# Loading the first weights from a second queue, turning the first rows by ordinary products, and an even last cut

## The chip, the cores and the metric

The kernel runs on one core of one Trainium2 chip. The time is device time of one execution, in microseconds; the kernel before was run three times (679.69, 679.70 and 680.63, median 679.7), and once more under the profiler (679.49, of which 677.7 are the profile's span).

## The reference

Two layers read the same x (2048 rows of 1024, bfloat16), and a gate mixes their results row by row.

```python
def _A_ref(x, wqkv, wo):            # attention, 32 heads of 32, window 8, step 2
    qkv = x @ wqkv
    ...
    attn = softmax(masked logits)
    return (sum over the window of attn * v) @ wo

def _B_ref(x, w_in, w_sp, b_sp, w_out):
    z = gelu(x @ w_in)              # w_in: 1024 x 3584
    z1, z2 = z[:, :1792], layernorm(z[:, 1792:])
    return (z1 * (w_sp @ z2 + b_sp)) @ w_out

g = sigmoid((x * gate_w).sum(-1))
out = g * _A_ref(x) + (1 - g) * _B_ref(x)
```

## The kernel before, in words

Everything on SBUF lives in one large tile, `arena`, in which regions are named and reused. PSUM is one pool of eight banks, tag `ps`. The kernel is written under a manual schedule: each engine runs its instructions in the order in which the program writes them, and each waits on semaphores for what it reads. TensorE goes through long runs of matrix products: x by the second half of w_in (line 300), x by wqkv (lines 621 and 644), x by the first half of w_in (line 809), w_sp by z2 (lines 836 and 910), and then the two output products, with w_out (line 1038) and with wo (lines 1117 and 1127).

The change touches the two ends.

*The front.* TensorE multiplies with the contraction on the partitions, so x is needed with its columns on the partitions: `xT`, of which each row tile of 128 rows has eight pieces of 128 columns (`kt`, eight row blocks of w_in). Row tiles 2 to 15 are turned by DMA (`dma_start_transpose`, line 523). Row tiles 0 and 1 are loaded as they lie, into `xn` (line 514), and turned by TensorE in `z2_quad` (line 316), four pieces to a PSUM bank; VectorE (line 320) and ScalarE (line 322) copy two pieces each into `xT`. While x's first tile is on its way, TensorE runs `warm_up`: seven products of constants (line 100).

`z2_quad` then makes four output banks at once: row tiles 0 and 1 (`i`) by column chunks 0 and 1 (`c`, 512 columns each) of w_in's second half. It runs over the eight row blocks `kt`, and in each over `c` and then `i`, so 32 products of 128x128 by 128x512. Block 0 comes in two transfers, one for each column chunk (line 516); blocks 1 to 7 come in one transfer each of 128 x 1024 values, 256 KB (line 518). Behind the quad, row tile 2 is taken up, then 3 and so on (`z2_tile`).

All these transfers are issued by SyncE, one after the other. A transfer tells of its landing by one of eight semaphores in turn, and each issue waits until the transfer eight places before it has landed.

*The end.* `both_pairs(7)` makes the last 256 output rows. The last product, `product4(..., a22, wo_sums[3], ...)` (lines 1190 to 1193), is done in two column parts of the last half row: 384 columns in the bank `apb`, and 128 in `apd`, into which ScalarE copied `apb`'s last 128 columns before (line 1176). VectorE's `combine` (line 1107) scales each part by the gate and adds it to `mix`, which ScalarE writes from the bank `mpb` just ahead (line 1181); SyncE stores each part by itself (line 1193).

## Time and profile before

| what | value |
|---|---|
| median of three runs | 679.7 us |
| the profiled execution | 679.49 us |
| its span | 677.7 us |
| TensorE busy | 673.0 us, 99% |
| VectorE busy | 558.4 us, 82% |
| ScalarE busy | 415.8 us, 61% |
| warm-up products | 0.78 to 3.61 us |
| x's first two tiles turned | 3.42 to 5.17 us |
| first product of line 300 | 5.69 us |
| last product of line 1127 begins to end | 673.23 to 674.27 us |

Times in the profile are counted from the start of the span. A row of the timeline shows start, length, engine, line, operation, output and input and the number of merged instructions; what stands in brackets is the idle time of the engine before it and what ended that. A row of the chain of waits shows start, length and what ran or was waited for. A row of a group shows output and input, form and count, then busy time in us, the mean of one in ns, and idle time before them. "PE" is TensorE's product, "PEld" its weight load, "SPq" and "ACTq" the issue of a transfer by SyncE and by ScalarE.

## The change

w_in's row block 0 becomes one transfer of 256 KB and is issued by ScalarE; the other seven stay with SyncE. Row tiles 0 and 1 are turned by ordinary products with the identity matrix in place of transposes, with float32 banks in place of bfloat16 ones. Row tile 0 is turned first and multiplied with block 0, then row tile 1 is turned, and the other products follow in the order tile 0 block 1, tile 1 blocks 0 and 1, and from block 2 on tile 0 and tile 1 in turn. At the end, the last product is cut into 256 and 256 columns, and ScalarE's copy ahead of it takes 256 columns.

```diff
     def z2_quad():
-        for i in range(2):
+        def turn(i):
             for h in range(2):
-                pt = psum.tile([P, 4, P], BF, name="pt", tag="ps")
+                pt = psum.tile([P, 4, P], F32, name="pt", tag="ps")
                 for k in range(4):
-                    nc.tensor.transpose(pt[:, k, :], xn[:, i, (4 * h + k) * P:(4 * h + k + 1) * P], ident[:])
+                    nc.tensor.matmul(pt[:, k, :], xn[:, i, (4 * h + k) * P:(4 * h + k + 1) * P], ident[:],
+                                     start=True, stop=True)
...
-        quad = [[psum.tile([P, 512], F32, name="ps", tag="ps") for c in range(2)] for i in range(2)]
-        for kt in range(KT):
+
+        turn(0)
+        quad = [[psum.tile([P, 512], F32, name="ps", tag="ps") for c in range(2)]]
+        order = [(0, 0), (0, 1), (1, 0), (1, 1)] + [(i, kt) for kt in range(2, KT) for i in range(2)]
+        for i, kt in order:
             for c in range(2):
-                for i in range(2):
-                    z2_mm(quad[i][c], i, c, kt, ZW[c])
+                z2_mm(quad[i][c], i, c, kt, ZW[c])
+            if (i, kt) == (0, 0):
+                turn(1)
+                quad.append([psum.tile([P, 512], F32, name="ps", tag="ps") for c in range(2)])
...
-    for c in range(2):
-        sync.dma_start(w2[c][:, 0, :], win_v[:, 0, FH + ZC * c:FH + ZC * (c + 1)])
-    for kt in range(1, KT):
-        sync.dma_start(w2_01[:, kt, :], win_v[:, kt, FH:FH + 2 * ZC])
+    for kt in range(KT):
+        queue = nc.scalar if kt == 0 else sync
+        queue.dma_start(w2_01[:, kt, :], win_v[:, kt, FH:FH + 2 * ZC])
...
         if q == 7:
             apd = bank()
-            nc.scalar.copy(apd[:, 384:512], apb[:, 384:512])
+            nc.scalar.copy(apd[:, 256:512], apb[:, 256:512])
...
-            for ps, n0, nw in ((apb, 0, 384), (apd, 384, 128)):
+            for ps, n0, nw in ((apb, 0, 256), (apd, 256, 256)):
                 product4(ps[:, n0:n0 + nw], a22, wo_sums[3][:, :, n0:n0 + nw], False)
                 combine(b, ps[:, n0:n0 + nw], n0, nw)
                 sync.dma_start(out2[b * P:(b + 1) * P, n0:n0 + nw], ob_slots[b % 4][:, n0:n0 + nw])
```

## What was predicted

> **What bounds the kernel now.** I read the page first, then the chain of waits in order of time, for its first 36 us and its last 5, then the timeline of those two stretches.

> ```profile
> span 677.7 us, 8946 instructions
> PE 673.0 (99%) x3311; PEld 355.1 (52%) x3311; DVE 558.4 (82%) x667; ACT 415.8 (61%) x765; POOL 29.4 (4%) x62
> PE 99%; DMA 1%; SPq 0%; ACT 0%; DVE 0%; issue 0%; DVEq 0%
> ```

> TensorE is busy for 673.0 of 677.7 us and makes up 99% of the chain. All that the change can win lies at the two ends, and the first is a DMA wait:

> ```profile
> 1.65 4.00 DMA arena<-in_B_w_in_dram
> 5.65 0.04 issue
> 5.69 1.02 PE ps L300 x4
> 6.71 0.02 issue
> 6.73 28.65 PE ps L300 x132
> ```

> Columns: start, length, what. The first half of w_in's row block 0 is issued at 1.65 and lands at 5.65; the first product of line 300 starts at 5.69. Four products later TensorE waits once more (the fifth starts at 6.73), then it runs without a hole at 28.65/132 = 0.217 us a product. The timeline of the same stretch:

> ```profile
> 0.73 1.28 ACT L322 ACT_TABLE_LOAD   x1 [0.73 <-PEq L1303]
> 0.74 0.87 SPq L514 DMA_DIRECT2D arena<-in_A_x_dram  x2
> 0.78 2.83 PE L100 MATMUL pw<-const-bfloat16-1.0 128*128 128x512 bf16 x7 [0.78 <-PEq L1303]
> 1.65 0.91 SPq L516 DMA_DIRECT2D arena<-in_B_w_in_dram  x2
> 2.60 3.40 SPq L518 DMA_DIRECT2D arena<-in_B_w_in_dram  x7
> 3.42 1.58 PEld L316 LDWEIGHTS <-arena 128*128 128x128 bf16 x16 [0.41 <-DMA arena<-in_A_x_dram]
> 3.42 1.75 PE L316 MATMUL pt<-ident,arena 128*128 128x128 bf16 x16
> 4.07 1.44 DVE L320 COPY arena<-pt 128x256 bf16<-128x256 bf16 x4 [4.07 <-PE pt L316]
> 4.39 1.52 ACT L322 COPY arena<-pt 128x256 bf16<-128x256 bf16 x4 [2.38 <-DVE arena L320]
> 6.06 9.22 SPq L523 DMA_TRANSPOSE arena<-in_A_x_dram  x5
> 12.50 2.57 DVE L528 TENSOR_REDUCE o_l<-arena 128x1 f32<-128x1024 bf16 x2 [4.74 <-DMA arena<-in_A_x_dram]
> ```

> x's first tile releases the turns at 3.42; the 16 turns are through at 5.17, and TensorE idles 0.52 us. The row at 12.50 is VectorE released by row tile 2, the first that a DMA turns: it has landed by 12.50. TensorE takes it up a little later:

> ```profile
> 12.34 0.81 PE L300 MATMUL ps<-arena 128*128 128x512 bf16 x3
> ```

> That is the 31st and 32nd product of the quad and then the first of tile 2, which starts at 12.34 + 2 x 0.217 = 12.77. So the front of the kernel is two races: TensorE reaches the end of its quad at 12.77, and the DMA stream delivers tile 2 at 12.50, only 0.27 us ahead. Mean DMA rates by stretch (last two columns: busy share, GB/s):

> ```profile
> 3.00:3.50 0.50, 0.50 (x4) 0.09 (x3) 0.00 (x0) 0.00 (x0) 0.02 (x1) 1.00 1.03 397
> 3.50:4.00 0.50, 0.50 (x7) 0.50 (x7) 0.00 (x0) 0.00 (x0) 0.00 (x0) 1.00 0.48 96
> 4.00:4.50 0.50, 0.50 (x8) 0.50 (x6) 0.29 (x2) 0.11 (x1) 0.00 (x0) 1.00 0.55 139
> 4.50:5.00 0.50, 0.50 (x8) 0.50 (x7) 0.37 (x2) 0.44 (x2) 0.00 (x0) 1.00 0.98 256
> 5.00:5.50 0.50, 0.18 (x3) 0.06 (x2) 0.50 (x3) 0.45 (x2) 0.00 (x0) 1.00 1.09 375
> ```

> The stream drops from 397 GB/s to 96 and 139 just where the first reads of w_in begin. Against 397 it loses (301 + 258 + 141) x 0.5 = 350 KB there, 0.88 us of its own pace.

> **The change, part by part.** *w_in's row block 0.* Two 128 KB transfers, issued third and fourth on SyncE's queue (1.65, some 0.47 apart), become one of 256 KB, issued first on ScalarE's. The instruction order puts it ahead of the table load: the load that starts at 0.73 starts some 0.4 later and ends near 2.4; the first copy that needs it starts at 4.39, so that costs nothing (0.4 us at most without that cover). On SyncE's queue the seven other blocks come two places, 0.91 us, earlier. Each issue there waits for the eighth transfer before it, so what SyncE waits for moves too: block 6 now waits for block 0, block 7 for x's first tile, and the first turning transfer of line 523 for x's second tile instead of the second half of block 0 (6.06). All three come earlier than they did, if ScalarE's transfer isn't late.

> When does block 0 land? No row shows a transfer on ScalarE's queue this early. Those of line 851 do it under load, at 512 KB each:

> ```profile
> L851 ACTq DMA_DIRECT2D arena<-in_B_w_sp_dram x4: 334/356/447, 362.6 to 369.5; - x4
> DMA to landing us min/median/max: 4.9/10.7/11.0
> ```

> Lower end: beside x's first tile, landing with it at 3.42. Upper end: 4.9 us after 0.74, at 5.64. The nearest row is the chain's 4.00 us for half of the very same rows; it includes a queue that the new place does not have, but half the bytes. I take it: 0.74 + 4.00 = 4.74.

> *x's first tile* now shares the 16 engines with block 0. Lower end: 3.42, as before. Upper end: all 256 KB pass ahead of it, 0.66 us at 397 GB/s, 4.08. Since the dip says that the first reads of w_in leave the engines half idle (0.48, 0.55), x loses less than its even share; I take 3.80.

> *The turns.* Sixteen transposes become sixteen products with the same weights and the same 128 moving columns; I price them alike, 1.75/16 = 0.11 us at the early pace. That pace is half of the later one, as the two means for one shape show:

> ```profile
> L100 PE MATMUL pw<-const-bfloat16-1.0 128*128 128x512 bf16 x6 | 2.7, 624 | 0.8 <-PEq L1303 0.8
> L300 PE MATMUL ps<-arena 128*128 128x512 bf16 x384 | 86.0, 379 | 0.5 <-DMA arena<-in_B_w_in_dram 0.5
> L320 DVE COPY arena<-pt 128x256 bf16<-128x256 bf16 x4 | 1.2, 292 | 4.3 <-PE pt L316 4.1
> L605 ACT CAST arena<-ps 128x256 bf16<-128x256 f32 x16 | 5.5, 380 | 4.6 <-PE ps L621 4.6
> ```

> (Warm-ups: 2.83 us for six and a quarter, 0.43 each, against 0.217.) The granted clock of the rows above reads 1.00 throughout and doesn't show this. PSUM now holds f32; the L605 row copies the same shape from f32 in 380 ns, against 1.52/4 = 380 for the old copies, so the copies cost the same on ScalarE. For VectorE I carry the same over (its copy: 292 ns); its dearest bound is the 384-wide pass over f32 of the last fence below, 0.62, or +0.33 on the path.

> *The order.* The first two products (tile 0, block 0) now follow the first eight turns; the second eight turns come behind them, and so does everything else on TensorE if block 0 is late. Before, the first copy ended 4.07 + 0.29 = 4.36, 0.94 after the first turn; with 0.04 for the semaphore the first product can start 0.98 after it: 3.80 + 0.98 = 4.78. Block 0 asks for 4.74 + 0.04 = 4.78 as well. From there: 2 x 0.217 + 8 turns at 0.07 (between 0.055, half the early pace, and 0.11) + 30 x 0.217 = 0.43 + 0.56 + 6.51 = 7.50. The quad ends at 12.28 instead of 12.77: 0.49 gained. With x at 3.42 and block 0 no later than 4.36 it would end at 11.90 (0.87 gained), with x at 4.08 at 12.56 (0.21). The second turns' copies have two products of block 1 and x's landing ahead of them and finish inside that work.

> This stands only if the stream keeps ahead. Block 1 is needed by 4.78 + 0.43 + 0.56 = 5.77 and lands now at about 6.7 (the wait that ends at 6.73); tile 2 is needed at 12.28 and lands at 12.50. Both must come earlier, by 0.9 and 0.2 us. For tile 2 a quarter of the 0.88 us lost in the dip does it. For block 1 it takes nearly all; what is missing there is a wait at that place, and the later blocks are then ahead of it again. I count 0.10 for it: front gain 0.39.

> [...]

> *The last product* is cut 256 + 256 instead of 384 + 128:

> ```profile
> 673.43 0.70 ACT arena L1181
> 674.15 0.62 DVE arena L1107
> 674.80 0.82 SPq L1193 DMA_DIRECT2D out_dram<-arena  x2
> L1193 SPq DMA_DIRECT2D out_dram<-arena x2: 333/362/391, 674.8 to 675.2; - x2
> L1107 DVE SCALAR_TENSOR_TENSOR arena<-ps,g_s,arena 128x384 bf16<-128x384 f32 x1 | 0.6, 617 | 1.5 <-ACT arena L1181 1.5
> L1107 DVE SCALAR_TENSOR_TENSOR arena<-ps,g_s,arena 128x128 bf16<-128x128 f32 x1 | 0.3, 341 | 0.0
> L1176 ACT COPY ps<-ps 128x128 f32<-128x128 f32 x1 | 0.2, 250 | 3.4 <-DVE arena L1107 3.4
> ```

> The first combine shrinks from 617 to (617 + 341)/2 = 479 ns, so the first store is issued 0.14 earlier; the second follows 0.82 - 0.39 = 0.43 behind it, as before, and its combine (0.48) is just done by then. The last store doubles to 64 KB: 0 to 32 KB/397 GB/s = 0.08 more. Gain 0.06 to 0.14, taken as 0.10. The copy of L1176 doubles its columns, about +0.13 us; ScalarE is idle until 673.43, which hides it (uncovered it would be 0.13).

> **Sum.** 0.39 + 0.10 = 0.49. The profiled execution took 679.49 us (677.7 of span, 1.8 around it) and becomes 679.0; the median shown, 679.7, lies 0.21 above it, so the forecast is 679.2.

> **The rivals.** *One: the stream is no faster.* The bytes up to tile 2 are the same, so it still lands at 12.50, and TensorE gains at most 0.27 in front however early it starts; with the end 0.37, less what x's delay costs: 679.4. For it: the rate between 5.00 and 5.50 is already 375 GB/s. Against it: the dip is latency, not bytes (engines half idle). Chance 0.20.

> *Two: block 0 lands late on the idle queue.* In the new order TensorE can't use the wait for the second turns. The quad ends at landing + 0.04 + 7.50, so it is a loss from a landing after 5.23. At 5.64 (the least of L851): 13.18, 0.41 lost, 0.10 won at the end: 680.0. Against it: L851's transfers are twice as big and run among others. Chance 0.10.

> *Three: slower, since TensorE's full pace comes later.* The pace doubled after 4.1 us of work without a gap (from 0.78; the turns still took 0.11 in the mean, the products at 5.69 came at 0.217). The change opens a hole between the last warm-up (ends 3.61) and the first turn at 3.80 to 4.08. If a hole restarts the count, full pace comes 4.1 us after 3.80, at 7.9: from 4.78 on 3.1 us run at half pace, 1.55 us lost, less 0.49: +1.1, 680.8; it decides from a doubling after 5.8, where the loss passes the gain. At x = 4.08 it is 1.55 - 0.21 - 0.10 = +1.2, 680.9. Against it: a hole of 0.2 to 0.47 us is small, and before had one of 0.52 at 5.17 without harm, though past the doubling. [...] Chance 0.14.

> **How the numbers follow.** Forecast (gain 0.2 to 0.9) 0.51, rivals 0.20, 0.10, 0.14, and 0.05 for a spread like that of the runs shown (680.63 beside 679.69). The likeliest is 679.2, its own range 678.8 to 679.5. The range 678.5 to 680.8 takes in the best front (0.87 + 0.14 against the median: 678.7) and rival three's nearer half; about 0.12 lies outside. A difference below 0.2% (1.36 us) can't be told from none here. The whole front can't win that, so faster is 0.03, from spread alone; slower is 0.10: the half of rival three that the spread of the runs lifts over the bound (0.07), a very late block 0 (0.02), spread (0.01). Within: 0.87.

> **What would show it.** Right: the first product of line 300 near 4.8 instead of 5.69, the turns in two groups of eight about it, rates above 200 GB/s in every half microsecond from 3.0, tile 2 taken up near 12.3, the last store issued near its old time less 0.6. Wrong: a PE wait on a DMA after the quad (rival one), a first product after 5.2 (two), products 0.43 apart after 5.5 (three). A VectorE copy of clearly over 0.3 us would upset the price of the turns.

## The result, and the profile after

The kernel after takes 680.94 us (median of 22 runs, 679.80 to 681.98), the kernel before beside it 679.75 us (22 runs, 679.40 to 680.63): a ratio of 1.0016, interval 1.0009 to 1.0022. That is slower by some 1.2 us, within the 0.2% that the prediction called no change, but 0.14 us above the top of its range. The times after lie in two heaps: 6 of 22 at 679.80 to 680.03, like before, and 16 from 680.83 up. The profiled execution (681.76 us) is one of the 16; it is 2.3 us longer than that of before.

The page of the kernel after, span and busy time:

```profile
span 680.0 us, 8945 instructions
PE 674.7 (99%) x3311; PEld 355.6 (52%) x3311; DVE 559.1 (82%) x667; ACT 415.9 (61%) x765; POOL 29.4 (4%) x62
```

TensorE's busy time grew by 1.7 us for the same 3311 instructions: most of the loss isn't idle time but slower work. The chain of waits after, in order of time (start, length, what), its first 37 us:

```profile
0.74 3.79 DMA arena<-in_A_x_dram
4.53 0.05 issue
4.58 0.62 PE pt L316 x4
5.20 0.02 issue
5.22 0.43 DVE arena L321
5.66 0.05 issue
5.70 1.03 PE ps L300 x2
6.74 0.85 PE pt L316 x8
7.59 29.61 PE ps L300 x132
```

The wait that ends last in front is no longer w_in's block 0 but x's first tile, which lands at 4.53. The timeline after, the same stretch:

```profile
0.74 0.88 SPq L520 DMA_DIRECT2D arena<-in_A_x_dram  x2
0.74 0.41 ACTq L523 DMA_DIRECT2D arena<-in_B_w_in_dram  x1
0.78 2.83 PE L100 MATMUL pw<-const-bfloat16-1.0 128*128 128x512 bf16 x7 [0.78 <-PEq L1308]
4.58 1.03 PE L316 MATMUL pt<-ident,arena 128*128 128x128 bf16 x8 [0.98 <-DMA arena<-in_A_x_dram]
9.10 0.15 PEld L300 LDWEIGHTS <-arena 128*128 128x128 bf16 x1 [0.28 <-issue]
9.52 0.15 PEld L300 LDWEIGHTS <-arena 128*128 128x128 bf16 x1 [0.28 <-issue]
9.84 4.42 PEld L300 LDWEIGHTS <-arena 128*128 128x128 bf16 x21 [0.17 <-issue]
11.59 3.52 DVE L533 TENSOR_REDUCE o_l<-arena 128x1 f32<-128x1024 bf16 x3 [1.28 <-DMA arena<-in_A_x_dram]
14.59 0.81 PE L300 MATMUL ps<-arena 128*128 128x512 bf16 x3
```

Two things are to be seen. TensorE is idle for 0.98 us between its warm-up and the first turn. And its weight loads for line 300 still come 0.43 us apart at 9.10 and 9.52; only then do 21 of them fit into 4.42 us, 0.21 each. Before, products ran at that pace from 5.69 on. Tile 2 has landed by 11.59, 0.9 earlier than before, but TensorE takes it up at 14.59 + 2 x 0.217 = 15.02 instead of 12.77. This 2.25 is all of the longer span: from there to the end both kernels take 665.0 us (680.0 - 15.02 and 677.7 - 12.77 = 664.9).

## The hole and the clock

The windows give the granted clock as 1.00 throughout, but the trace also holds a record of when TensorE's clock goes from half to full, and back near the end (in before a share of 1.0 from 4.91 on and of 0.5 from 677.33, 3.06 after the last product's end; ahead of 4.91 it has no entry, and the warm-up's weight loads come 0.43 us apart). For all the profiles of this case (the experiments are told below), in us from the start of the span, with TensorE's idle time in the last window that failed to open the clock and in the one that did (time in which no product or turn ran; what lies before the span's start counts as idle):

```
kernel               full at  half at  apart    idle, window before   idle, window that opened
after                  9.73   678.74   669.01   1.07                  0.00
before                 4.91   677.33   672.42   2.70                  0.00
e1_long_warm_up        4.20   676.62   672.42   3.41                  0.00
e2_products_only       5.48   677.91   672.43   2.12                  0.06
e3_queue_only          9.67   678.68   669.01   0.84                  0.00
e4_block0_on_sync      9.54   678.55   669.01   0.90                  0.00
e5_end_only            6.14   678.56   672.42   1.46                  0.00
e6_short_warm_up       6.82   679.24   672.42   1.44                  0.34
e7_after_transposes    8.08   680.50   672.42   1.05                  0.00
e8_x0_w0_x1_fill       3.56   679.40   675.84   -                     0.62
e9_first_touch         4.19   680.02   675.83   3.41                  0.00
e10_before_filled      4.32   676.75   672.43   3.28                  0.00
e11_half_hole          3.91   679.75   675.84   -                     0.28
e12_touch_all          5.96   678.38   672.42   1.64                  0.17
```

The time between the two changes takes only three values, 669.01, 672.42 and 675.84, which lie 3.41 apart and are 196, 197 and 198 times 3.4133. So I read the openings, by estimate from these 14 profiles, as falling on a grid of 3.41 us whose phase differs from run to run: where no hole comes between, they lie anywhere from 3.56 to 6.14, though the warm-up begins at 0.77 or 0.78 (seen in 13 of the 14). The paces bear the records out: after's weight loads are 0.43 us apart up to 9.52 and 0.21 from 9.84 on, about its record at 9.73. Counting windows of 3.41 us back from each opening, the clock opened in each profile at the end of the first window in which TensorE was idle for at most 0.62 us (the most is e8's), and never at the end of one with 0.84 (e3's) or more. In after, e3, e4 and e7 the window that failed holds a hole (0.84 to 1.07 idle), in e6 a hole and the start; the others failed for the idle time ahead of the first warm-up product alone. After's windows were 2.90 to 6.31, which holds the whole hole (3.61 to 4.58), and 6.31 to 9.73, which opened it.

This also accounts for the two heaps, by estimate from these numbers: the hole does no harm only where a boundary of the grid lies between 3.57 (0.78 - 0.62 + 3.41, little enough idle before the warm-up) and 4.23 (3.61 + 0.62, little enough of the hole). That is 0.66 of 3.41, a fifth of all phases; 6 of 22 runs took no longer than before. Elsewhere the opening is put off to 7.6 to 10.4 (4.23 + 3.41, and 3.57 + 2 x 3.41). At half pace from the first product at 5.70 on, that costs half of the time up to the opening, 1.0 to 2.3 us; the upper heap, 680.83 to 681.98, lies 1.0 to 2.1 above the middle of the lower one (679.88).

## The experiments

Each was timed in five rounds (11 runs) beside the kernel before; its runs in the four groups had medians 679.84, 679.79, 679.84 and 679.77. "Above 680.3" counts the runs of the upper heap; of the 22 runs of before above, 4 lie there.

**The hole closed, x still late.** Of the kernel after, only the warm-up is longer:

```diff
-    warm_up((512,) * 6 + (128,))
+    warm_up((512,) * 8 + (256,))
```

> The changed kernel with eight and a half warm-up products of 512 in place of six and a quarter, so that TensorE works until about 4.4 us and the hole before x's first tile (lands at 4.53) is closed. Theory one (the hole of 0.98 us put off the doubling of TensorE's pace from 4.9 to 9.7): the pace doubles near 5 us again, and the time falls from 680.9 to 679.7 to 680.2; what is left over the kernel before is x's delay. Theory two (x's delay alone is the price, and the late doubling is chance): the time stays within 0.3 of 680.9 and the doubling moves at random. Theory three (products with the identity don't count as work for the clock, whatever the warm-up): the doubling stays after 8 us, the time at 680.9.

Measured: 679.77 us (679.66 to 680.15), ratio 0.9999 [0.9990, 1.0008], 0 of 11 above 680.3. Its timeline:

```profile
0.78 3.67 PE L100 MATMUL pw<-const-bfloat16-1.0 128*128 128x512 bf16 x9 [0.78 <-PEq L1308]
4.61 0.62 PE L316 MATMUL pt<-ident,arena 128*128 128x128 bf16 x8 [0.16 <-DMA arena<-in_A_x_dram]
5.97 0.61 PE L316 MATMUL pt<-ident,arena 128*128 128x128 bf16 x8
```

x comes as late as in the kernel after (4.61), but eight turns take 0.62 us instead of 1.03: the pace has doubled already. The loss is the hole's, not x's delay.

**The products alone, and the queue alone.** Both are edits of the kernel before: products into float32 banks for the transposes in their old order, or only the new transfer of block 0.

```diff
-                pt = psum.tile([P, 4, P], BF, name="pt", tag="ps")
+                pt = psum.tile([P, 4, P], F32, name="pt", tag="ps")
...
-                    nc.tensor.transpose(pt[:, k, :], xn[:, i, (4 * h + k) * P:(4 * h + k + 1) * P], ident[:])
+                    nc.tensor.matmul(pt[:, k, :], xn[:, i, (4 * h + k) * P:(4 * h + k + 1) * P], ident[:],
+                                     start=True, stop=True)
```

> The kernel before, with nothing changed but the sixteen transposes turned into products with f32 banks. Theory one: no hole, so the pace doubles near 4.9 as before; VectorE's copies take 0.42 instead of 0.29 us, hidden behind the wait for w_in: 679.6 to 679.9. Theory two: the same. Theory three: the doubling comes after 8 us and the time rises by 1 us or more, to 680.7 to 681.5.

Measured: 679.84 us (679.62 to 680.68), 1.0000 [0.9991, 1.0008], 3 of 11 above 680.3. Products or transposes: no difference.

```diff
-    for c in range(2):
-        sync.dma_start(w2[c][:, 0, :], win_v[:, 0, FH + ZC * c:FH + ZC * (c + 1)])
-    for kt in range(1, KT):
-        sync.dma_start(w2_01[:, kt, :], win_v[:, kt, FH:FH + 2 * ZC])
+    for kt in range(KT):
+        queue = nc.scalar if kt == 0 else sync
+        queue.dma_start(w2_01[:, kt, :], win_v[:, kt, FH:FH + 2 * ZC])
```

> The kernel before, with nothing changed but w_in's row block 0 as one transfer on ScalarE's queue. Theory one: x's first tile lands near 4.5, the hole opens, the pace doubles late in most runs, 680.4 to 681.4. Theory two: x lands near 4.5, sixteen turns at 0.11 end near 6.3, the quad near 13.3: +0.5, 680.2, with the doubling near 5 in the profile. Theory three: as theory two, the products are not there.

Measured: 680.82 us (679.51 to 681.54), 1.0010 [1.0001, 1.0019], 7 of 11 above 680.3. Its timeline:

```profile
0.78 2.83 PE L100 MATMUL pw<-const-bfloat16-1.0 128*128 128x512 bf16 x7 [0.78 <-PEq L1302]
4.45 1.89 PE L316 MATMUL pt<-ident,arena 128*128 128x128 bf16 x16 [0.84 <-DMA arena<-in_A_x_dram]
9.12 0.15 PEld L300 LDWEIGHTS <-arena 128*128 128x128 bf16 x1 [0.28 <-issue]
9.54 4.70 PEld L300 LDWEIGHTS <-arena 128*128 128x128 bf16 x22 [0.28 <-issue]
```

The queue by itself makes the hole (0.84) and the late doubling (9.67): this one transfer is enough for the loss, without the new order and without the products.

**Block 0 back on SyncE.** The kernel after, with `queue = sync` for all blocks, so that x comes early again.

```diff
-        queue = nc.scalar if kt == 0 else sync
+        queue = sync
```

> The changed kernel with w_in's row block 0 as one transfer, but third on SyncE's queue. x's first tile lands at 3.4, so there is no hole before the first turn; block 0 lands near 5.7 to 6.0 and the second turns stand behind it: the quad ends at 5.9 + 7.5 = 13.4, 0.6 later than before. Theory one: the pace doubles near 5 (at the latest one step later in some runs, since TensorE idles from 4.3 to 5.9), 680.2 to 680.9, with spread. Theory two: 680.3. Theory three: the doubling after 8 us, 681.5 or more.

Measured: 679.95 us, 1.0011 [1.0001, 1.0020]; six runs at 679.70 to 679.95, five at 681.28 to 682.27. Its timeline:

```profile
3.45 1.04 PE L316 MATMUL pt<-ident,arena 128*128 128x128 bf16 x8
5.38 1.01 PE L300 MATMUL ps<-arena 128*128 128x512 bf16 x2 [0.90 <-DMA arena<-in_B_w_in_dram]
9.58 4.63 PEld L300 LDWEIGHTS <-arena 128*128 128x128 bf16 x22 [0.25 <-issue]
```

x is in time (3.45), but in the new order the second eight turns can't fill the wait for block 0: the hole is only moved, to 4.48 to 5.38, and spoils the window there (0.90 idle). So a hole of that size does it in this place too, and x needn't be late. By the reckoning above, this hole does no harm for a boundary between 3.57 and 5.10 (4.48 + 0.62), 0.45 of all phases by estimate; 6 of 11 runs show no loss.

**The end alone.** The kernel before with the last product cut 256 + 256.

```diff
-            nc.scalar.copy(apd[:, 384:512], apb[:, 384:512])
+            nc.scalar.copy(apd[:, 256:512], apb[:, 256:512])
...
-            for ps, n0, nw in ((apb, 0, 384), (apd, 384, 128)):
+            for ps, n0, nw in ((apb, 0, 256), (apd, 256, 256)):
```

> The kernel before with only the last product cut 256 + 256. From the changed kernel's trace, the first combine is 0.14 shorter, but from its start to the end of the span it takes 3.6 us there and took 3.6 before: 679.6 to 679.9, no difference. By the prediction's term: 0.10 less, 679.7. A rival that puts part of the loss at the end: 680.0 or more.

Measured: 679.69 us, 0.9996 [0.9987, 1.0005]: nothing that can be told from zero, nor from the 0.10 of the prediction. The chain of waits of the kernel after shows how little is to be had:

```profile
675.68 0.70 ACT arena L1186
676.38 0.03 issue
676.40 0.48 DVE arena L1112
676.88 0.39 DVEq L1319
```

The first combine takes 0.48 instead of 0.617 us, as reckoned, but from its start to the end of the span it is 680.0 - 676.40 = 3.6 us, and before 677.7 - 674.15 = 3.55. The 0.14 is mostly given back by the second, larger store: by the trace's semaphores and counted from the first combine's start, its issue begins 0.94 later instead of 1.07, but it lands 1.61 after its issue instead of 1.52, so that the landing comes 0.04 sooner (2.55 instead of 2.59; the same 2.55 in the run of the end alone).

**A hole without touching a transfer.** The kernel before, with two warm-up products less.

```diff
-    warm_up((512,) * 6 + (128,))
+    warm_up((512,) * 4 + (128,))
```

> The kernel before with two warm-up products of 512 less: TensorE stops near 2.7 and x's first tile lands at 3.4 as before, so there is a hole of 0.7 to 0.9 us and nothing else is changed. Theory one (a hole ahead of the first turn puts the doubling of the pace off by one step): runs in two or three groups, the median 680.3 to 681.0, late doubling in the profile in half of the cases or more. Rival (only x's delay costs; chance decides the doubling): 679.8, the same spread as before.

Measured: 680.44 us (679.62 to 681.15), 1.0005 [0.9996, 1.0014], 7 of 11 above 680.3, where before beside it had 4 of 33. The interval holds 1, so the ratio alone doesn't settle it; the counts speak for a cost of the hole. Its timeline, of a run of 679.81 us:

```profile
0.77 1.97 PE L100 MATMUL pw<-const-bfloat16-1.0 128*128 128x512 bf16 x5 [0.77 <-PEq L1303]
3.50 1.89 PE L316 MATMUL pt<-ident,arena 128*128 128x128 bf16 x16 [0.75 <-DMA arena<-in_A_x_dram]
6.43 0.15 PEld L300 LDWEIGHTS <-arena 128*128 128x128 bf16 x1 [0.28 <-issue]
```

A hole of 0.75 and, with the 0.77 before the first warm-up, a window from 0.0 to 3.4 that is idle for 1.44; the products are still slow at 6.43. This profile doesn't single out the hole: 0.77 alone lies between the 0.62 and the 0.84 of above, and the opening at 6.82 costs the run little.

**After with transposes.** The kernel after, turned by transposes into bfloat16 banks again (the reverse of the first diff under "the products alone").

> The changed kernel with transposes in place of the products with the identity. Theory one: the hole is there still, 680.6 to 681.3, runs in groups as in the changed kernel. Rival (transposes don't count as work for the clock, so the products saved something): more late runs, 681.3 to 682.0. Rival (the products are what puts it off): 679.8 to 680.2.

Measured: 680.92 us (679.37 to 681.75), 1.0012 [1.0003, 1.0021], 7 of 11 above 680.3: the loss of the kernel after. By these profiles the transposes count as work for the clock: in the kernel before the window that opened it (1.49 to 4.91) holds nothing but transposes from 3.61 on, where the warm-up ends (1.30 us, which would be idle time if they didn't count, more than the 0.84 that kept a window shut), and here that of 4.66 to 8.08 holds all sixteen.

**The other order of loads.** The kernel after, everything on SyncE in the order x's first tile, block 0, x's second tile, the rest, and one warm-up product behind the first turns.

```diff
+        warm_up((512,))
...
-    for i in range(2):
-        sync.dma_start(xn[:, i, :], x_v[:, i, :])
-    for kt in range(KT):
-        queue = nc.scalar if kt == 0 else sync
-        queue.dma_start(w2_01[:, kt, :], win_v[:, kt, FH:FH + 2 * ZC])
+    sync.dma_start(xn[:, 0, :], x_v[:, 0, :])
+    sync.dma_start(w2_01[:, 0, :], win_v[:, 0, FH:FH + 2 * ZC])
+    sync.dma_start(xn[:, 1, :], x_v[:, 1, :])
+    for kt in range(1, KT):
+        sync.dma_start(w2_01[:, kt, :], win_v[:, kt, FH:FH + 2 * ZC])
```

> The changed kernel with all transfers on SyncE's queue in the order x's first tile, w_in's block 0 in one transfer, x's second tile, the other blocks; and one more warm-up product of 512 between the first eight turns and the first product of line 300. x's first tile lands at 3.4, no hole before the turns and a short one after them, so by theory one the pace doubles near 5 in nearly all runs; block 0 lands at 4.6 to 5.1, the quad ends at 5.0 + 7.5 = 12.5 against 12.77: 679.3 to 679.7. By the rival that only the stream counts (same bytes, tile 2 at 12.5): 679.5 to 679.8. Worse than 679.9: block 0 is later than 5.3 or a hole is left.

Measured: 679.76 us (679.09 to 680.42), 0.9997 [0.9988, 1.0006]. That is no faster than before, above the 679.3 to 679.7 expected and inside the range of the rival (only the stream counts): in its timeline the second turns now wait 1.41 us, for x's second tile.

```profile
6.56 0.62 PE L316 MATMUL pt<-ident,arena 128*128 128x128 bf16 x8 [1.41 <-DMA arena<-in_A_x_dram]
```

**The slow first reads of w_in.** The kernel before, with a transfer of 4 bytes of each row of block 0 first on ScalarE's queue (into a tile that nothing reads); and the same with 4 bytes of each row of all eight blocks.

```diff
+    touch = sm.tile([P, 2], BF, name="touch")
...
+    nc.scalar.dma_start(touch[:], win_v[:, 0, FH:FH + 2])
```

> The kernel before, with one more transfer ahead of everything on ScalarE's queue: four bytes of each row of w_in's block 0, into a small tile that nothing reads. It tests why the stream drops between 3.5 and 4.5. If the drop is the delay of the first reads of these rows (the theory behind w_in's share of x's delay), it is gone or halved, block 0's first half lands before 5.2, the first product of line 300 comes near 5.2 with no hole after the turns, and the time is 679.2 to 679.6. If the first reads take as long but are paid by x instead, x lands 0.3 to 1 us later and the time is 679.8 to 680.8. If the drop has nothing to do with first reads: block 0 lands at 5.3 to 5.7 as before, 679.7 to 679.9.

Measured: 679.58 us (679.17 to 680.13), 0.9993 [0.9984, 1.0002]: as expected, though the time alone can't be told from before's. The windows of this run (last two columns: DMA busy share, GB/s):

```profile
3.50:4.00 0.50, 0.50 (x6) 0.49 (x6) 0.00 (x0) 0.00 (x0) 0.00 (x0) 1.00 1.00 354
4.00:4.50 0.50, 0.44 (x6) 0.26 (x3) 0.32 (x2) 0.01 (x1) 0.00 (x0) 1.00 0.94 240
```

Where before moved 96 and 139 GB/s, it moves 354 and 240. So the dip goes with the first reads of these rows, not with the bytes; why a first read is slow, no run shows. By the trace's semaphores the first half of block 0 lands at 4.80 instead of 5.65, while x's second tile pays a part (4.51 instead of 4.00). Block 1, untouched, is then the one that is late (7.38 instead of 6.69); the timeline of the same run:

```profile
5.01 1.22 PE L300 MATMUL ps<-arena 128*128 128x512 bf16 x4
7.42 7.07 PE L300 MATMUL ps<-arena 128*128 128x512 bf16 x32 [1.19 <-DMA arena<-in_B_w_in_dram]
```

```diff
+    touch = sm.tile([P, KT, 2], BF, name="touch")
...
+    nc.scalar.dma_start(touch[:], win_v[:, :, FH:FH + 2])
```

> The kernel before with the small transfer of the last experiment taking four bytes of every row of all eight blocks of w_in. There, block 0 came 0.85 earlier, but block 1 landed at 7.4 and TensorE waited 1.2 us for it. If each block's first reads are slow once, the wait for block 1 goes too: quad 0.3 to 0.6 earlier than before, 679.1 to 679.5. If 1024 small reads hold up x instead: x's first tile lands after 4, a hole opens, 680 or more.

Measured: 679.08 us (678.87 to 679.73), 0.9991 [0.9982, 1.0000], the best median of the study, 0.7 us under before beside it; its interval ends at 1.0000, so the gain is likely rather than sure. Block 1 lands at 6.10, and in its timeline no DMA wait is left from the first product on:

```profile
5.54 9.01 PE L300 MATMUL ps<-arena 128*128 128x512 bf16 x40
```

**Before, its own hole filled.** The kernel before with two warm-up products between the turns and the first product, where it idles 0.52 us.

```diff
+        warm_up((512, 256))
```

> The kernel before, with one and a half warm-up products more between its sixteen turns and its first product of line 300, where it idles for 0.5 us. If holes are what puts the doubling off, the slower runs of the kernel before (680.4 and more, about a quarter) get rarer: 679.5 to 679.8 and no run above 680.3. If a hole of 0.5 us never matters: 679.8, the same spread as before.

Measured: 679.78 us (679.40 to 680.29), 0.9997 [0.9988, 1.0006]; 0 of 11 above 680.3, where before beside it had 7 of 27. By chance alone that happens once in some 25 times ((20/27) to the eleventh is 0.04), so it hints at a cost of that hole and doesn't show it. A hole of 0.52 alone would spoil no window by the limits above, so what makes the slower runs of before stays open.

**Half a hole.** The kernel after with one warm-up product more.

```diff
-    warm_up((512,) * 6 + (128,))
+    warm_up((512,) * 7 + (128,))
```

> The changed kernel with seven and a quarter warm-up products of 512, so that the hole before x's first tile is halved (TensorE works until about 4.0, x lands at 4.5). If a hole counts by its length: between the changed kernel (680.9) and the one with the hole closed (679.8), 679.9 to 680.5. If any hole at all restarts the count: 680.9. If only a hole of more than half a microsecond counts: 679.7 to 679.9.

Measured: 679.96 us, 1.0006 [0.9996, 1.0017]; six runs at 679.41 to 679.96, one at 680.53, four at 681.49 to 681.93. Its timeline:

```profile
0.78 3.25 PE L100 MATMUL pw<-const-bfloat16-1.0 128*128 128x512 bf16 x8 [0.78 <-PEq L1308]
4.66 0.62 PE L316 MATMUL pt<-ident,arena 128*128 128x128 bf16 x8 [0.63 <-DMA arena<-in_A_x_dram]
5.57 0.60 PE L300 MATMUL ps<-arena 128*128 128x512 bf16 x2 [0.30 <-DVE arena L321]
```

The profiled run (679.76) belongs to the six. A window that held both gaps, 0.63 and 0.30, would be idle for 0.93, more than any that opened the clock. By estimate a boundary from 5.5 to 6.98 (3.57 + 3.41), 0.43 of all phases, ends a window with 0.84 or more; 4 of 11 runs are long. That this made them long is inferred, since no trace of them is there.

## Why the prediction was wrong, and where it was right

The sum failed in two terms that hang together: the landing of x's first tile, and, by the hole that it opened, the pace of the products, which the sum took at 0.217 us from 4.78 on.

*x's first tile: the step that failed first.* The prediction took 3.80 and, as upper end, 4.08; measured 4.53. It let x wait for the 256 KB of block 0 at most. The windows, TensorE alone (busy, granted clock, DMA share, GB/s), of the kernel after:

```profile
1.50:2.00 0.50, 0.50 (x2) 1.00 0.62 33
2.00:2.50 0.50, 0.50 (x3) 1.00 0.31 119
2.50:3.00 0.50, 0.50 (x3) 1.00 0.82 279
3.00:3.50 0.50, 0.50 (x3) 1.00 0.98 381
3.50:4.00 0.50, 0.10 (x1) 1.00 1.04 397
4.00:4.50 0.50, 0.00 (x0) 1.00 1.10 402
```

and of the kernel before:

```profile
1.50:2.00 0.50, 0.50 (x2) 1.00 0.61 53
2.00:2.50 0.50, 0.50 (x3) 1.00 0.70 176
2.50:3.00 0.50, 0.50 (x3) 1.00 1.05 402
```

Up to 4.50 the kernel after moved (33 + 119 + 279 + 381 + 397 + 402) x 0.5 = 806 KB, about as much as block 0 and both tiles of x together. The three came in side by side: by the trace's semaphores x's first tile landed at 4.53, block 0 at 4.71 and x's second tile at 5.27 (before: x's tiles at 3.38 and 4.00). When x's first tile landed before, some 466 KB had moved by the same rows, so the 350 KB more cost 0.88 us at 397, where the bound counted 0.66 for block 0 alone: by estimate some 90 KB of the other transfers passed ahead as well. On top comes a slower start: 33, 119 and 279 GB/s against 53, 176 and 402, which is 100 KB less by 3.00, or 0.25 us at 397. The two make 1.13 of the 1.15 us. The bound had no term for the slower start, though the same prediction had read the dip at 3.5 as slow first reads; that this dip moved to 2.0 with block 0 is likely, but no run tests it there.

*The pace, and rival three: the right mechanism, held for unlikely.* The sum itself had no term for a late doubling. The argument against the rival was that a hole of 0.2 to 0.47 us is small, and for such a size the profiles bear it out: windows with up to 0.62 us of idle time opened the clock. It fell with x's landing, since the hole became 0.98, and the rival's sign, products 0.43 apart after 5.5, is what the trace shows. Its rule was off: a hole didn't restart a count of 4.1 us (7.9); in after, e3, e4 and e7 the window of 3.41 us that held it (0.84 to 1.07 idle) didn't open the clock and the next one did, so the opening comes, by the estimate above, anywhere from 7.6 to 10.4 (8.08, 9.67 and 9.73 in the profiles with block 0 on the new queue and no longer warm-up), and in some runs isn't late at all. That its time, 680.8, lies so near the 680.94 measured is partly chance: it had a smaller delay of x and an earlier doubling, and no run without loss.

*The sum, mended.* First product 4.78 + 0.78 (x lands so much later than taken, 4.58 for the first turn instead of 3.80) + 0.14 (copy) = 5.70, as measured. From there 9.32 to tile 2 instead of 7.50: 1.82 lost at half pace. 12.28 + 0.78 + 0.14 + 1.82 = 15.02.

*The copy.* VectorE's copy from float32 was priced as the old one, 292 ns, with 0.62 us as bound. The groups of the kernel after:

```profile
L321 DVE CAST arena<-pt 128x256 bf16<-128x256 f32 x4 | 1.7, 425 | 6.4 <-PE pt L316 6.3
L323 ACT CAST arena<-pt 128x256 bf16<-128x256 f32 x4 | 1.5, 372 | 4.5 <-DVE arena L321 4.4
```

and ScalarE's old copy, of the kernel before:

```profile
L322 ACT COPY arena<-pt 128x256 bf16<-128x256 bf16 x4 | 1.4, 372 | 2.5 <-DVE arena L320 2.4
```

425 ns, 0.13 more on the path; ScalarE's copies do cost the same, as the prediction said, though at 372 ns (its 380 for the old ones is 1.52/4 and holds the gaps between them). A second slip changes nothing: 2.83 us for six and a quarter warm-up products is 0.45 each, not 0.43.

*Right:* block 0 landed at 4.71, taken as 4.74, and didn't make TensorE wait; a product turns at the price of a transpose (1.03/8 = 0.13 at the early pace beside 0.11 taken, the same 1.03 for e7's first eight transposes, and no change in time when exchanged); the stream ran ahead (tile 2 by 11.59), so the first rival, a stream no faster, and the second, a late block 0, were false. Of the 0.10 at the end the trace shows 0.04 and the times nothing; the 0.10 set aside for block 1 wasn't needed: at TensorE's slow pace nothing waited for it. With the clock opened in time, but x as late as here, the new front gains nothing that can be told from zero: the longer warm-up puts the kernel after at 0.9999 of before. What it would be worth with x at 3.80, no run shows.

## What to carry to other kernels

Here the first few microseconds decided when TensorE reached full pace: with a warm-up that ended at 3.61 and an input that landed at 4.53, 16 of 22 runs were above 680.3, and with one that ended at 4.45, 0 of 11. So let a warm-up last until the first input really lands, with margin, and where an edit makes that input land later, lengthen the warm-up in the same edit. The second queue brought no second stream: with it 402 GB/s were reached at best up to 4.50, without it 402 as well, and the block issued beside the input needed first delayed it by 1.15 us, more than the 0.66 of its bytes. Where a change moves the time by 0.2%, look at the heaps in the runs before the median; here they pointed to a phase.
